# A new order of the attention's steps, and one row-sum step fewer per head pair

## The chip, the cores and the metric

The kernel runs on one core of a Trainium2 chip. A core has five engines, each with its own queue that is worked off in order: TensorE (PE in the profile; PEld are its weight loads), VectorE (DVE), ScalarE (ACT), GpSimd (POOL) and SyncE (SP), which here only issues DMAs. The metric is the time of one execution in microseconds on the device. Before the change it is 854.01 us, the median of three runs (853.5 to 854.5).

## The reference

Three parts follow one another: attention with a memory term over 4 batches of 8 heads, 576 positions and 64 columns, then two feed-forward layers over its output as 2304 tokens of 512 columns.

```python
scores = scale * np.matmul(q, k.transpose(0, 1, 3, 2))
scores = np.where(causal, -1000000000.0, scores)
scores = scores - scores.max(-1, keepdims=True)
a = np.exp(scores)
a /= a.sum(-1, keepdims=True) + 1e-09
local = np.matmul(a, v)
...
q_p = phi(q)                       # where(x > 0, x, exp(x) - 1) + 1
mem_out = (q_p @ M_prev) / (q_p @ z_prev + 1e-6)
return g * mem_out + (1 - g) * local     # g = sigmoid(beta), per head
```

The layers take weights of 64-bit floats, which arrive as pairs of 32-bit integers and are put together on the chip from exponent and mantissa.

## The kernel before

The attention works on 16 pairs of heads. Each pair runs through some seventy steps; a step is a method that issues a few instructions, nearly always on one engine. The steps that matter, with the pair as their argument n:

- lq, lk, lv, lz, cv_d: loads of q, k, v and M, z, and of raw weights, all issued on SP. tq_p, tk_p: transposes of q and k on TensorE; tq_h, tk_h (ScalarE) and tq_l, tk_l (VectorE, lines 393 and 406) split them into a high and a low part.
- s0_p to s4_p: scores on TensorE, block i having 128 (i + 1) columns, block 4 the 64 last rows of both heads. s0_m to s4_m: mask and row maximum on VectorE, reading PSUM (line 496). s0_e to s4_e: exponential with row sums on ScalarE (line 502). n01_r, n23_r, n4_r: a reduce and a reciprocal of a few columns on VectorE (lines 506 and 507). n0_p to n4_p: each block times its reciprocal on GpSimd, in place (line 513): two operations of 128, 256, 384 or 512 columns, one of 576 for block 4.
- ph_e: exp(q) on ScalarE (line 411). ph_m: minimum and maximum-plus on VectorE (lines 415 and 416, 640 columns, within SBUF). ph_g: times z on GpSimd (line 419). ph_r: row sum and reciprocal on VectorE (lines 427 and 428). ph_s: times the reciprocal on GpSimd (line 436). tf_p, tf_c: transpose and copy.
- g0_p, g1_p, t0_p to t3_p, tt_p, tc_p: transposes of the normalized blocks on TensorE; g1_c, tc_c (VectorE) and the other _c steps (ScalarE) copy them from PSUM. x0_m, x1_m, a00 to a14: products with M and v; x0_c, x1_c: copies of the result on VectorE.
- cv_a, cv_r, cv_b, cv_l: the conversion of raw weights of the first layer, beside the attention. For an even n these are exponent (line 194), bias on ScalarE (199), upper (202) and rest (209); for an odd n power (212, cv_a) and lower (215, cv_b). All but the bias are VectorE operations on 512 integers within SBUF.

Nothing is scheduled at run time. The lists HEAD, ORDER and TAIL at the top of the file give the order in which steps are issued, as name and pair. ORDER is repeated for a loop index and its numbers are relative to that; BODY is the loop's range, (1, 12), so eleven times. The order of the list is the order in each engine's queue; between engines only the data counts, so a step on GpSimd starts as soon as its own queue and its inputs allow, wherever the list has it. After the attention come the two layers, whose code the change does not touch; the first tiles of the first layer (xs0, xs1, h0 to h11, mx, ex, mu, sq, nm) stand in TAIL.

Of the kernel before, what the change touches and what calls it, by code (L numbers as in the profile page):

```python
# [22 lines left out]
HEAD = """
lq:0 ph_e:0 ph_m:0 tq_p:0 tq_h:0 tq_l:0 lk:0 lz:0 tk_p:0 tk_h:0 tk_l:0 s0_p:0 cv_h:0 s0_m:0 s4_p:0 lz:1
s4_m:0 lq:1 ph_g:0 ph_r:0 tq_p:1 tq_h:1 tq_l:1 s4_e:0 n4_r:0 ph_s:0 n4_p:0 s1_p:0 s1_m:0 s1_e:0 s3_p:0 s3_m:0
lk:1 tk_p:1 tk_h:1 s2_p:0 lz:2 s3_e:0 lq:2 tk_l:1 s3_p:1 s2_m:0 s2_e:0 n23_r:0 s0_e:0 n01_r:0 n1_p:0 cv_d:0
s0_p:1 n3_p:0 tf_p:0 n2_p:0 tf_c:0 s0_m:1 s4_p:1 lk:2 ph_e:1 s4_m:1 s4_e:1 g1_p:0 g1_c:0 ph_m:1 ph_g:1 lq:3
s0_e:1 s1_p:1 s1_m:1 s1_e:1 s2_p:1 s2_m:1 t3_p:0 tt_p:0 tt_c:0 t3_c:0 lv:0 ph_r:1 ph_s:1 tk_p:2 tk_h:2 cv_a:0  # L30
tq_p:2 cv_r:0 n4_r:1 n4_p:1 tk_l:2 tq_h:2 tc_p:0 lk:3 tc_c:0 n0_p:0 t1_p:0 t1_c:0 tq_l:2 tf_p:1 tf_c:1 t2_p:0
s4_p:2 s3_m:1 t2_c:0 n01_r:1 n0_p:1 s4_m:2 ph_e:2 cv_b:0 g0_p:0 lz:3 g0_c:0 t0_p:0 t0_c:0 s2_e:1 n1_p:1 s2_p:2
ph_m:2 ph_g:2 s1_p:2 s1_m:2 s0_p:2 s0_m:2 x0_m:0 a01:0 cv_d:1 x1_m:0 a00:0 s3_e:1 n23_r:1 n2_p:1 n3_p:1 s2_m:2
a14:0 a13:0 s1_e:2 a12:0 cv_p:0 a11:0 s4_e:2 a10:0 x1_c:0 ph_r:2 ph_s:2 tt_p:1 tt_c:1 tc_p:1 tc_c:1 tq_p:3
tq_h:3 tk_p:3 x0_c:0 t3_p:1 t1_p:1 s3_p:2 s0_e:2 t3_c:1
""".split()


TAIL = """
s3_m:13 cv_d:13 g0_p:12 s2_e:13 g0_c:12 lv:12 x1_m:12 a14:12 a13:12 n4_r:13 t1_c:12 cv_d:15 tq_l:14 s3_e:13 g1_p:12 g1_c:12  # L40
n01_r:13 n23_r:13 t0_p:12 n1_p:13 tk_h:14 tk_l:14 cv_a:12 n4_p:13 t0_c:12 x0_m:12 a01:12 cv_h:14 a00:12 n2_p:13 t2_p:12 x0_c:12
tf_p:13 t2_c:12 lv:14 s1_p:14 s1_m:14 s0_p:14 tf_c:13 a12:12 a11:12 a10:12 ph_e:14 s0_m:14 s0_e:14 s1_e:14 s2_p:14 n3_p:13
t2_p:13 t2_c:13 ph_m:14 x1_c:12 s2_m:14 s2_e:14 ph_g:14 ph_r:14 lz:15 xs0:0 tc_p:13 tc_c:13 s4_p:14 s4_m:14 t1_p:13 t1_c:13
cv_r:12 lq:15 tq_p:15 lk:15 s3_p:14 s3_m:14 t3_p:13 tq_h:15 t3_c:13 lv:13 tt_p:13 cv_b:12 cv_h:15 ph_s:14 tf_p:14 n01_r:14
n0_p:13 s4_e:14 n1_p:14 cv_r:13 tq_l:15 cv_l:12 g0_p:13 tt_c:13 g0_c:13 cv_h:13 x1_m:13 ph_e:15 a14:13 n0_p:14 g1_p:13 g1_c:13
cv_l:11 t0_p:13 tk_p:15 n4_r:14 n4_p:14 ph_m:15 ph_g:15 s3_e:14 tk_h:15 n23_r:14 n2_p:14 t0_c:13 n3_p:14 x0_m:13 cv_p:15 a13:13
a12:13 a11:13 tf_c:14 tk_l:15 cv_a:13 cv_b:13 a01:13 a00:13 x0_c:13 cv_d:14 cv_a:14 cv_r:14 a10:13 x1_c:13 s2_p:15 s0_p:15
s0_m:15 xs1:0 s4_p:15 tt_p:14 s4_m:15 tc_p:14 tt_c:14 tc_c:14 cv_b:14 s3_p:15 s3_m:15 s1_p:15 s1_m:15 s2_m:15 xs0:1 s0_e:15
t1_p:14 g0_p:14 x1_m:14 a14:14 g0_c:14 t2_p:14 s1_e:15 n01_r:15 n0_p:15 cv_p:12 ph_r:15 ph_s:15 cv_l:14 h0:0 h1:0 cv_r:15
t1_c:14 h2:0 h3:0 g1_p:14 h4:0 h5:0 h6:0 n1_p:15 cv_a:15 g1_c:14 h7:0 s2_e:15 h8:0 cv_p:14 s3_e:15 n23_r:15  # L50
cv_l:15 n2_p:15 cv_b:15 t2_c:14 s4_e:15 n4_r:15 t0_p:14 tf_p:15 tf_c:15 x0_m:14 a01:14 a00:14 cv_d:16 cv_a:16 cv_d:17 cv_a:17
cv_r:16 cv_b:16 t3_p:14 h0:1 n3_p:15 t0_c:14 xs1:1 n4_p:15 tt_p:15 h1:1 h9:0 tt_c:15 h10:0 cv_r:17 h11:0 cv_b:17
cv_p:17 lv:15 t2_p:15 mx:0 t2_c:15 h2:1 h3:1 cv_p:16 tc_p:15 t3_c:14 xs0:2 xs1:2 h4:1 tc_c:15 cv_h:12 ex:0
x0_c:14 g0_p:15 g0_c:15 cv_d:18 t1_p:15 t1_c:15 a13:14 cv_d:19 mu:0 a12:14 a11:14 a10:14 x1_c:14 cv_h:17 cv_l:17 cv_a:19
sq:0 g1_p:15 g1_c:15 cv_r:19 h5:1 h6:1 h7:1 cv_h:16 cv_l:16 cv_a:18 h8:1 h9:1 h10:1 cv_p:13 h11:1 cv_r:18
cv_b:19 t3_p:15 t3_c:15 nm:0 mx:1 cv_b:18 ex:1 t0_p:15 t0_c:15 mu:1 cv_p:18 cv_h:18 x0_m:15 a01:15 a00:15 x0_c:15
cv_p:19 cv_h:19 cv_l:18 cv_l:13 sq:1 x1_m:15 a14:15 a13:15 a12:15 a11:15 a10:15 cv_l:19 nm:1 x1_c:15
""".split()
# [1367 lines left out]
```

## Time and profile before

| | |
|---|---|
| median of three runs | 854.01 us |
| the profiled execution | 853.87 us, its span 852.1 us |
| TensorE busy | 829.5 us (97%) |
| VectorE busy | 636.8 us (75%) |
| ScalarE busy | 463.7 us (54%) |
| GpSimd busy | 478.4 us (56%) |
| head of the attention | 0 to 40.2 us |
| its eleven body periods | 40.2 to 170.8 us |
| its tail, with the first layer's first tiles | 170.8 to about 228.8 us |

The shares are means over stages of different kinds. The span runs from the first to the last instruction. In a timeline, a row is an instruction or several alike that follow each other; the number behind it in brackets is the time that the engine sat idle before it, and what released it.

### The profile page before, as it was taken

How to read it: one execution, taken by the hardware profiler on the slowest of the kernel's cores; microseconds unless marked ns; L12 is line 12 of the kernel's file. 1: busy time of each engine (PE TensorE's matmuls, PEld its weight loads, DVE VectorE, ACT ScalarE, POOL GpSimd, SP SyncE). 2: the span in 40 equal slices, each digit the busy share in tenths (PEclk: the TensorE clock that was granted, in tenths of full speed). 3: DMA queues.
4: the chain of work that ended last, by engine and by line, in shares of the span. 5: the costliest groups of instructions: out<-in, count | busy, mean ns of one | idle time of the engine just before them, and what ended most of it. 6: DMA issues, size and time to landing. Idle time of an engine off the chain costs nothing.

```text
span 852.1 us, 14791 instructions
## 1 busy us (share of the span) xinstructions
PE 829.5 (97%) x5020; PEld 730.3 (86%) x5020; DVE 636.8 (75%) x1340; ACT 463.7 (54%) x971; POOL 478.4 (56%) x563
## 2 busy tenths in 40 slices
...
GB/s 150 91 147 138 139 151 161 140 102 103 75 65 60 143 187 172 204 184 144 81 278 325 252 182 300 403 333 113 335 401 291 258 209 101 112 380 40 244 237 99
DMA packets 135835, 160.37 MB, mean 188 GB/s; under 512 B 69840, under 2 KB 103888, under 8 KB 135760
## 3 DMA queue, kind: packets, MB, share of 16 engines
...
q14 instruction: 35, 0.29, 0.1%
q10 hardware_dynamic: 320, 0.07, 0.0%
...
## 4 chain that ended last, share of the span: by engine, by line
PE 55%; DVE 6%; ACT 5%; POOL 4%; DMA 2%; issue 2%; SPq 0%; POOLq 0%; ACTq 0%; DVEq 0%
PE s L1169 17%; PE acc L1222 16%; PE g L1169 8%; PE po L816 7%; PE v L1169 4%; PE h L750 2%; ACT h L779 1%; DVE e L774 1%; DMA raw<-in_moe_w_val_dram 1%; ACT e L768 1%; DMA gv0s<-scrg 1%; POOL exwo L721 1%; POOL M L1016 1%; PE pl L797 1%; POOL M L1002 1%
## 5 line engine op out<-in xcount | busy, mean ns | idle before, releaser
L1222 PE MATMUL acc<-o,G 128*128 128x512 f32 x648 | 181.6, 390 | 0.2 <-DVE G L1188 0.2
L1207 POOL TENSOR_TENSOR vl<-vl,sg 128x384 f32<-128x384 f32 x36 | 37.1, 1030 | 204.4 <-ACT sg L1206 204.4
L1222 PEld LDWEIGHTS acc<-o,G 128*128 128x128 f32 x648 | 118.5, 188 | 10.3 <-DVE G L1188 0.7
L513 POOL TENSOR_SCALAR p<-p,first,cols 128x256 f32<-128x256 f32 (+4 forms) x142 | 105.7, 757 | 36.5 <-ACT p L502 14.3
L502 ACT ACTIVATE p<-p,nm 128x256 f32<-128x256 f32 (+4 forms) x144 | 83.1, 581 | 14.3 <-DVE nm L496 14.2
L750 PE MATMUL h<-wih,xs 128*128 128x512 f32 x288 | 84.5, 398 | 0.3 <-POOL xs L739 0.2
L1199 ACT ACTIVATE sg<-sg 128x384 f32<-128x384 f32 x36 | 18.9, 526 | 105.5 <-DVE sg L1198 105.4
L816 PE MATMUL po<-lnT,woh 128*128 128x384 f32 x288 | 73.5, 335 | 1.9 <-ACT woh L726 1.9
L1188 DVE TENSOR_TENSOR G<-vl,G 128x384 fp32r<-128x384 f32 x72 | 54.4, 755 | 21.5 <-ACT G L1185 21.4
L1185 ACT CAST G<-vl 128x384 fp32r<-128x384 f32 x72 | 37.1, 515 | 45.3 <-POOL vl L1207 36.4
L750 PEld LDWEIGHTS h<-wih,xs 128*128 128x128 f32 x288 | 52.3, 188 | 10.7 <-POOL xs L739 0.6
L1206 ACT ACTIVATE sg<-sg 128x384 f32<-128x384 f32 x36 | 18.9, 526 | 74.6 <-DVE sg L1205 74.5
L816 PEld LDWEIGHTS po<-lnT,woh 128*128 128x128 f32 x288 | 52.0, 188 | 2.6 <-ACT woh L726 2.3
L1002 POOL TENSOR_TENSOR M<-ex 128x256 f32<-128x256 f32 x48 | 42.3, 901 | 18.4 <-DVE ex L167 18.4
L816 PE MATMUL po<-lnT,wol 128*128 128x384 f32 x144 | 48.3, 335 | 0.2 <-DVE wol L727 0.2
L1193 DVE TENSOR_TENSOR u<-s,p 128x384 f32<-128x384 f32 x36 | 20.0, 557 | 36.6 <-PE s L1169 36.6
L750 PE MATMUL h<-wil,xs 128*128 128x512 f32 x144 | 44.9, 393 | 0.0
L1016 POOL TENSOR_TENSOR M<-M 128x256 f32<-128x256 f32 x48 | 43.8, 922 | 1.2
L1210 POOL TENSOR_TENSOR vl<-vl,sg 128x384 f32<-128x384 f32 x36 | 41.0, 1140 | 2.2 <-DVE vl L1209 0.5
L1209 DVE TENSOR_TENSOR vl<-v,u 128x384 f32<-128x384 f32 x36 | 20.1, 559 | 28.3 <-PE v L1169 28.2
L160 ACT ACTIVATE ex<-ex,consts 128x512 int32<-128x512 int32 x36 | 26.0, 722 | 28.0 <-DVE ex L150 28.0
L163 DVE SCALAR_TENSOR_TENSOR ex<-raw,ex 128x512 int32<-128x512 int32 x36 | 33.4, 928 | 10.2 <-ACT ex L160 10.2
...
## 6 DMA issues: line engine op xcount, KB each, us to landing
...
```

Source lines behind the costliest of these rows:

```text
L502: nc.scalar.activation(p, p, AF.Exp, bias=nm, scale=-1.0, accum_out=self.sum[n % 2][:, c, 0:1])
L513: eng.tensor_scalar(p, p, r["rs"][:, c : c + 1], og, ALU.mult, ALU.mult)
L750: lambda s=s, w=w, j=j: nc.tensor.matmul(ph[:, j * 512 : j * 512 + 512], xs[:, s, c], self.wi[c][w][:, j * 512 : j * 512 + 512], start=(c ...
L816: nc.tensor.matmul(self.po[g, m], w[:, m * P : m * P + P], L[x][c // 4][:, c % 4], start=(c == 0 and n == 0), stop=(c == NF1 - 1 and n == 2),)
L1002: nc.gpsimd.tensor_mul(out[:, sl], m[:, sl], e[:, sl])
L1016: ops[i][0](*ops[i][1:])
L1169: nc.tensor.matmul(po, W[:, a, c * P : c * P + P], xb[b][:, c], start=c + i == 0, stop=c == 1 and i == 2)
L1185: nc.scalar.copy(G[:, 0, hs[h]], vl[:, h])
L1188: nc.vector.tensor_sub(G[:, 1, hs[h]], vl[:, h], f32(G[:, 0, hs[h]]))
L1207: nc.gpsimd.tensor_mul(vl[:, 1], vl[:, 1], sg[:, 1])
L1210: nc.gpsimd.tensor_mul(vl[:, 0], vl[:, 0], sg[:, 0])
L1222: nc.tensor.matmul(po, G[:, x, sl], o[:, w], start=first and i == 0, stop=stop and i == 2)
```

## The change

The three lists are new, and BODY is (2, 12): ten repeats. In ORDER the numbers run from -2 to 2 where they ran from -1 to 3. HEAD has 113 steps in place of 152, TAIL 393 in place of 286. The steps n23_r and n4_r become one, n24_r, which sums and inverts columns 4 to 8 at once, so that n2_p to n4_p all wait for one step. On VectorE the new period is: s4_m, n24_r, x0_c, cv_b, x1_c, s0_m, s1_m, s2_m, ph_r, cv_l, tc_c, tq_l, n01_r, tk_l, s3_m, ph_m, g1_c, cv_a. On GpSimd: n3_p, n4_p, n2_p, ph_s, n1_p, n0_p, ph_g. Before it was, on VectorE: tq_l, cv_a, tk_l, n01_r, cv_l, g1_c, s3_m, n4_r, cv_b, s4_m, n23_r, ph_m, x1_c, x0_c, s0_m, s1_m, s2_m, ph_r, tc_c; on GpSimd: n0_p, n1_p, n4_p, n3_p, ph_g, n2_p, ph_s. HEAD and TAIL are left out here.

```diff
-BODY = (1, 12)
+BODY = (2, 12)
...
 ORDER = """
-tq_l:2 t2_p:0 tf_p:1 tk_h:2 t1_c:0 cv_a:0 g1_p:0 t2_c:0 s2_e:1 tk_l:2 cv_p:0 lv:0 n01_r:1 cv_l:-1 s4_p:2 cv_h:0
-g1_c:0 g0_p:0 ph_e:2 s3_m:1 cv_r:0 lq:3 s3_e:1 t0_p:0 x1_m:0 n4_r:1 t0_c:0 a14:0 a13:0 cv_b:0 g0_c:0 a12:0
-x0_m:0 n0_p:1 s4_m:2 n1_p:1 s4_e:2 a11:0 tf_c:1 a01:0 a10:0 n23_r:1 n4_p:1 n3_p:1 ph_m:2 a00:0 s0_p:2 s1_p:2
-s2_p:2 ph_g:2 x1_c:0 x0_c:0 s0_m:2 s3_p:2 n2_p:1 s0_e:2 s1_m:2 s1_e:2 t3_p:1 t3_c:1 cv_d:1 tq_p:3 tt_p:1 lk:3
-tq_h:3 s2_m:2 tc_p:1 tt_c:1 tk_p:3 ph_r:2 tc_c:1 t1_p:1 lz:3 ph_s:2
+a12:-2 s3_e:-1 s4_m:0 lk:1 n24_r:-1 t0_c:-2 a01:-2 a00:-2 a11:-2 a10:-2 x0_c:-2 n3_p:-1 lq:2 s0_p:0 cv_r:-2 n4_p:-1
+n2_p:-1 tf_c:-1 cv_b:-2 s1_p:0 s4_e:0 x1_c:-2 s2_p:0 cv_d:-1 s0_m:0 s1_m:0 s3_p:0 s0_e:0 s2_m:0 ph_r:0 ph_s:0 t3_p:-1
+cv_p:0 tt_p:-1 s1_e:0 cv_l:-2 lz:2 t3_c:-1 lv:1 cv_h:0 tt_c:-1 tq_p:1 t1_p:-1 tq_h:1 t1_c:-1 tc_p:-1 tc_c:-1 tk_p:1
+tq_l:1 tk_h:1 t2_p:-1 t2_c:-1 n01_r:0 tk_l:1 s3_m:0 g0_p:-1 tf_p:0 t0_p:-1 g0_c:-1 s4_p:1 n1_p:0 ph_e:1 g1_p:-1 x0_m:-1
+ph_m:1 g1_c:-1 x1_m:-1 cv_a:-1 s2_e:0 a14:-1 a13:-1 n0_p:0 ph_g:1
 """.split()
...
 
             sub = {
                 "n01_r": lambda n, r: self.n_r(n, r, 0, 4),
-                "n23_r": lambda n, r: self.n_r(n, r, 4, 8),
-                "n4_r": lambda n, r: self.n_r(n, r, 8, 9),
+                "n24_r": lambda n, r: self.n_r(n, r, 4, 9),
             }
             for i in range(5):
                 sub[f"s{i}_p"] = lambda n, r, i=i: self.s_p(n, r, i)
```

## Rows read from the trace of the kernel before

**Rows 1.** Table by stretch (length, busy PE, PEld, DVE, ACT, POOL, clock, DMA)

```profile
40.20:170.80 130.60, 129.97 (x1166) 100.00 (x1167) 127.68 (x400) 118.33 (x317) 103.46 (x122) 1.00 0.56 144
170.80:228.80 58.00, 55.48 (x405) 40.15 (x404) 50.51 (x137) 43.46 (x99) 34.83 (x44) 1.00 0.32 93
```

**Rows 2.** Timeline of VectorE in the body (start, duration, line, operation)

```profile
100.24 0.81 DVE L393 SCALAR_TENSOR_TENSOR q<-trq,q 128x640 fp32r<-128x640 f32 x1
...
100.97 0.84 DVE L194 TENSOR_SCALAR exh<-rawh 128x512 int32<-128x512 int32 x1
...
101.73 0.75 DVE L406 TENSOR_TENSOR kl<-trk,kh 128x576 fp32r<-128x576 f32 x1
...
102.67 0.40 DVE L222 COPY A<-t6a 128x256 f32<-128x256 f32 x1
...
102.98 0.68 DVE L496 CUSTOM_DVE_ANT_0 p<-x7s,mask 128x512 f32<-128x512 f32 x1
...
104.20 0.15 DVE L506 TENSOR_REDUCE first<-cols 128x1 f32<-128x2 f32 x1
...
104.38 0.16 DVE L507 RECIPROCAL first<-first 128x1 f32<-128x1 f32 x1
...
106.37 0.46 DVE L415 TENSOR_SCALAR E<-E 128x640 f32<-128x640 f32 x1
...
106.87 1.28 DVE L416 SCALAR_TENSOR_TENSOR E<-qt,E 128x640 f32<-128x640 f32 x1
...
108.07 0.81 DVE L222 COPY X<-x 128x320 f32<-128x320 f32 x2
...
112.11 0.81 DVE L393 SCALAR_TENSOR_TENSOR q<-trq,q 128x640 fp32r<-128x640 f32 x1
```

**Rows 3.** Timeline of ScalarE in the body

```profile
97.33 0.40 ACT L502 ACTIVATE p<-p,nm 128x128 f32<-128x128 f32 x1 [1.29 <-DVE nm L496]
...
109.20 0.40 ACT L502 ACTIVATE p<-p,nm 128x128 f32<-128x128 f32 x1 [0.79 <-DVE nm L496]
```

**Rows 4.** Timeline of VectorE elsewhere, the same kinds of operation

```profile
5.52 0.82 DVE L416 SCALAR_TENSOR_TENSOR E<-qt,E 128x640 f32<-128x640 f32 x1
...
34.19 0.87 DVE L416 SCALAR_TENSOR_TENSOR E<-qt,E 128x640 f32<-128x640 f32 x1
...
90.80 0.40 DVE L209 TENSOR_SCALAR midh<-midh 128x512 int32<-128x512 int32 x1
```

**Rows 5.** Timeline of GpSimd, head and body

```profile
34.38 1.11 POOL L513 TENSOR_SCALAR p<-p,first,cols 128x256 f32<-128x256 f32 x1
...
106.66 2.14 POOL L513 TENSOR_SCALAR p<-p,first,cols 128x512 f32<-128x512 f32 x2 [0.50 <-ACT Bt L222]
...
112.13 1.26 POOL L436 TENSOR_TENSOR E<-E,nr 128x640 f32<-128x640 f32 x1 [0.50 <-DVE nr L428]
...
114.82 3.21 POOL L513 TENSOR_SCALAR p<-p,first,cols 128x128 f32<-128x128 f32 x5 [1.43 <-ACT p L502]
```

**Rows 6.** Timeline of GpSimd, tail and later

```profile
181.06 1.57 POOL L419 TENSOR_TENSOR G<-E,zm 128x640 f32<-128x640 f32 x1 [0.75 <-DVE E L416]
...
191.05 1.73 POOL L419 TENSOR_TENSOR G<-E,zm 128x640 f32<-128x640 f32 x1
...
206.94 1.36 POOL L513 TENSOR_SCALAR p<-p,first,cols 128x576 f32<-128x576 f32 x1
...
363.64 0.74 POOL L1030 TENSOR_TENSOR M<-M,hi 128x256 fp32r<-128x256 f32 x1
```

**Rows 7.** Timeline of VectorE at those places

```profile
179.70 1.27 DVE L416 SCALAR_TENSOR_TENSOR E<-qt,E 128x640 f32<-128x640 f32 x1
...
191.40 1.93 DVE L215 SCALAR_TENSOR_TENSOR wil<-midh,exh 128x512 fp32r<-128x512 int32 x1
...
207.02 0.40 DVE L163 SCALAR_TENSOR_TENSOR qt<-raw,qt 128x256 int32<-128x256 int32 x1
...
363.76 1.17 DVE L163 SCALAR_TENSOR_TENSOR ex<-raw,ex 128x512 int32<-128x512 int32 x1 [0.51 <-ACT ex L160]
```

More of the change, by code (lines that the diff above doesn't have):

```diff
@@ L18 @@
 PSUM = bass.MemoryType.PSUM
-BODY = (1, 12)
+BODY = (2, 12)
 HEAD = """
[L26 to L34, printed above, removed]
@@ L35 @@
-tq_h:3 tk_p:3 x0_c:0 t3_p:1 t1_p:1 s3_p:2 s0_e:2 t3_c:1
+lq:0 tq_p:0 ph_e:0 lk:0 ph_m:0 lz:0 ph_g:0 tq_h:0 tq_l:0 tk_p:0 tk_h:0 tk_l:0 s0_p:0 ph_r:0 s1_p:0 s1_m:0
+s1_e:0 s2_p:0 s2_m:0 lq:1 ph_s:0 s2_e:0 tf_p:0 tf_c:0 s4_p:0 s0_m:0 cv_h:1 ph_e:1 lz:1 tq_p:1 cv_p:0 lz:2
+s4_m:0 ph_m:1 ph_g:1 s4_e:0 cv_d:0 tq_h:1 tq_l:1 lk:1 tk_p:1 tk_h:1 cv_p:1 s3_p:0 tk_l:1 s1_p:1 lv:0 s3_m:0
+s3_e:0 cv_h:0 s1_m:1 s1_e:1 s2_p:1 s2_m:1 n24_r:0 n4_p:0 s3_p:1 s0_p:1 s0_m:1 lq:2 s0_e:0 n01_r:0 s0_e:1 n2_p:0
+tq_p:2 lv:2 tq_h:2 ph_r:1 tt_p:0 tt_c:0 s4_p:1 lk:2 n3_p:0 t3_p:0 n0_p:0 n1_p:0 lq:3 s3_m:1 n01_r:1 tq_l:2
@@ L36 @@
+t1_p:0 t1_c:0 tk_p:2 lv:1 s4_m:1 t3_c:0 cv_a:0 lz:3 ph_s:1 tf_p:1 tk_h:2 tk_l:2 tc_p:0 x1_m:0 x0_m:0 s4_e:1
+n1_p:1 tc_c:0 a14:0 ph_e:2 a13:0 ph_m:2 ph_g:2 s2_e:1 t2_p:0 t2_c:0 g0_p:0 g0_c:0 n0_p:1 s4_p:2 g1_p:0 g1_c:0
+t0_p:0
 """.split()
 TAIL = """
-s3_m:13 cv_d:13 g0_p:12 s2_e:13 g0_c:12 lv:12 x1_m:12 a14:12 a13:12 n4_r:13 t1_c:12 cv_d:15 tq_l:14 s3_e:13 g1_p:12 g1_c:12
-n01_r:13 n23_r:13 t0_p:12 n1_p:13 tk_h:14 tk_l:14 cv_a:12 n4_p:13 t0_c:12 x0_m:12 a01:12 cv_h:14 a00:12 n2_p:13 t2_p:12 x0_c:12
@@ L42 @@
[L42 to L54, printed above, removed]
@@ L55 @@
-sq:0 g1_p:15 g1_c:15 cv_r:19 h5:1 h6:1 h7:1 cv_h:16 cv_l:16 cv_a:18 h8:1 h9:1 h10:1 cv_p:13 h11:1 cv_r:18
-cv_b:19 t3_p:15 t3_c:15 nm:0 mx:1 cv_b:18 ex:1 t0_p:15 t0_c:15 mu:1 cv_p:18 cv_h:18 x0_m:15 a01:15 a00:15 x0_c:15
-cv_p:19 cv_h:19 cv_l:18 cv_l:13 sq:1 x1_m:15 a14:15 a13:15 a12:15 a11:15 a10:15 cv_l:19 nm:1 x1_c:15
+s4_m:12 t0_c:10 lk:14 a12:10 a11:10 s3_e:11 n24_r:11 tf_c:11 s4_e:12 cv_l:13 s1_p:12 s1_m:12 s1_e:12 n3_p:11 s0_p:12 s0_m:12
+cv_l:15 s2_p:12 s2_m:12 a01:10 a00:10 s2_e:12 a10:10 x0_c:10 x1_c:10 lk:13 n4_p:11 tc_p:11 tc_c:11 tt_p:11 ph_r:12 ph_s:12
@@ new lines @@
+cv_l:10 tt_c:11 tq_p:13 tq_h:13 tq_l:13 lq:14 n2_p:11 t3_p:11 tk_p:13 lk:15 lz:14 tk_h:13 t3_c:11 tk_l:13 g0_p:11 g0_c:11
+cv_h:14 s3_p:12 s3_m:12 s0_e:12 tf_p:12 tf_c:12 n01_r:12 cv_h:15 s4_p:13 g1_p:11 n1_p:12 g1_c:11 s3_e:12 t2_p:11 tq_p:14 s4_m:13
+n24_r:12 n3_p:12 tq_h:14 tq_l:14 t1_p:11 ph_e:13 ph_m:13 lq:15 t1_c:11 t2_c:11 x1_m:11 a14:11 a13:11 x0_m:11 t0_p:11 cv_r:10
+cv_b:10 s1_p:13 s1_m:13 t0_c:11 s2_p:13 s2_m:13 s1_e:13 s2_e:13 s0_p:13 s0_m:13 ph_g:13 ph_r:13 a12:11 a11:11 a10:11 x1_c:11
@@ new lines @@
+n4_p:12 a01:11 tt_p:12 tt_c:12 t3_p:12 t3_c:12 n0_p:12 a00:11 x0_c:11 n2_p:12 s0_e:13 t2_p:12 t2_c:12 t1_p:12 t1_c:12 tk_p:14
+tk_h:14 cv_d:13 cv_p:15 cv_h:13 cv_a:11 tc_p:12 tc_c:12 ph_s:13 tf_p:13 tf_c:13 n01_r:13 t0_p:12 t0_c:12 g0_p:12 xs0:0 tk_l:14
+s2_p:14 cv_b:11 s2_m:14 s4_e:13 s3_p:13 n0_p:13 s3_m:13 ph_e:14 ph_m:14 s4_p:14 g0_c:12 s3_e:13 n24_r:13 cv_p:12 tq_p:15 n2_p:13
+cv_d:12 cv_a:12 ph_g:14 tq_h:15 tq_l:15 lv:14 g1_p:12 x0_m:12 g1_c:12 s4_m:14 s4_e:14 x1_m:12 a14:12 xs1:0 a13:12 a12:12
@@ new lines @@
+a11:12 a10:12 x1_c:12 tk_p:15 s0_p:14 s0_m:14 s1_p:14 lv:13 tk_h:15 tk_l:15 cv_d:11 s1_m:14 s2_e:14 a01:12 cv_r:11 a00:12
+x0_c:12 n4_p:13 tt_p:13 n3_p:13 tt_c:13 n1_p:13 t2_p:13 s4_p:15 ph_r:14 t2_c:13 cv_r:12 cv_b:12 tc_p:13 tc_c:13 g0_p:13 g0_c:13
+s4_m:15 s3_p:14 s3_m:14 t1_p:13 t1_c:13 t3_p:13 t3_c:13 ph_s:14 tf_p:14 t0_p:13 g1_p:13 g1_c:13 x1_m:13 a14:13 a13:13 xs0:1
+s3_e:14 n24_r:14 n3_p:14 ph_e:15 ph_m:15 x0_m:13 a01:13 cv_a:13 tf_c:14 a12:13 n4_p:14 lv:15 cv_r:13 t0_c:13 a11:13 a10:13
```

11 lines of the change are left out of this document (added).

## The prediction

> **What bounds the kernel now.** The table by stretch first. The eleven body periods fill 40.2 to 170.8 us, 130.6 us, and VectorE is busy for 127.68 of them; the tail of the attention follows, 58.0 us with VectorE busy for 50.51 [rows 1]. The page warns that a busy TensorE is not TensorE at its peak, so I looked next at VectorE's own timeline. One period there, from tq_l to the next tq_l, is 100.24 to 112.11, 11.87 us, and each row starts about 0.08 before the one ahead of it ends: VectorE has no idle time worth naming [rows 2]. ScalarE does: 1.29 us in one period and 0.79 in the next, waiting for VectorE [rows 3], so alone it would need 11.87 - 1.04 = 10.83. The body is bound by VectorE, and a microsecond taken from its period is worth ten (the new order has ten body periods; the eleventh goes to the tail), until ScalarE binds.
>
> **What the change removes.** Three terms, from start to start, since that is what the next operation sees.
>
> ph_m: its second operation takes 1.28 in the body and 0.82 at the start of the kernel, where GpSimd is idle [rows 2, 4]. In the body it meets n3_p, two operations of 512 columns in 2.14 [rows 5]. The new order puts n1_p and n0_p in front of ph_m, and the end of n0_p may reach into it; beside such narrow operations ph_m's took 0.87, and it was GpSimd that waited, 1.11 for 256 columns at 34.38 [rows 4, 5]. Gain 0.41 (0.46 if n0_p is done).
>
> cv_a: 100.97 to 101.73 is 0.76; a like operation on 512 integers with GpSimd nearly idle takes 0.40, so 0.32 from start to start [rows 2, 4]. It meets ph_s now: the ph_s of 112.13 [rows 5] stands one period earlier at 100.26, ends at 101.52, and cv_a ends 0.29 later, at 101.81. Possible gain 0.44.
>
> n24_r: a reduce and a reciprocal fall away, 104.20 to 104.54, about 0.27 after the overlap [rows 2]; five columns should cost what four do.
>
> Together 1.12, so 10.75 a period: ScalarE's 10.83 would bind, and with queues in order I would take 11.0. That is the change at its word.
>
> **What it adds.** An order holds nobody back; GpSimd starts whenever its inputs are there. So I laid the new order out from these rows, with the end of ph_m as zero. GpSimd's queue there is n1_p, n0_p, ph_g. n1_p is released by n01_r; from that to the end of ph_m VectorE has tk_l 0.67, s3_m 1.22 (102.98 to 104.20) and ph_m 0.50 + 0.79, together 3.18 [rows 2, 4]. n1_p and n0_p are four of the five operations that take 3.21 [rows 5]; the fifth, n4_p, is the widest, so the four take at most 2.5. GpSimd is idle when ph_m ends, and ph_g starts at once: a ph_g that waited for ph_m started at 181.06, 0.09 after the end at 180.97 [rows 6, 7].
>
> VectorE's next are g1_c, which reads PSUM, and then cv_a. A copy of g1_c's size takes 0.31 from start to start (102.67 to 102.98) [rows 2] and starts 0.08 early, so cv_a comes at +0.23, 0.14 behind ph_g. Who goes first? At 191.05 a ph_g was running, and a VectorE operation of 191.40 ended at 193.33, 0.55 after ph_g [rows 6, 7]. At 363.64 GpSimd led by 0.12, and VectorE's operation was held until 364.93, 0.55 after GpSimd's end. At 206.94 GpSimd led by 0.08 and VectorE won: 0.40, and GpSimd's 576 columns took 1.36 [rows 6, 7]. So the lead decides, between 0.08 and 0.12, and 0.14 goes to GpSimd. cv_a then ends 0.29 after ph_g, whose 1.57 end at +1.66; the next operation starts at +1.87, so cv_a costs 1.6 where it cost 0.76. That is +0.84: the collision that was removed comes back in another place, larger. Ends of this term: -0.44 (cv_a first) and +0.9. I take +0.84, as the row nearest in lead has it. Behind cv_a are queued s4_m and n24_r, and ScalarE (s4_e) and GpSimd (n3_p) wait for those.
>
> cv_b: n3_p is released by n24_r some 0.2 after it, and cv_b follows n24_r and x0_c, at +0.23 to +0.26: a lead of 0.03 to 0.06, which goes to VectorE by the row of 207.02. Taken 0. If it goes to GpSimd, cv_b waits for one 512-wide operation, 0.6 (ends: -0.05 and +0.7).
>
> The page "SBUF — State Buffer" of the Trainium skill (Who interferes with whom) says that the port pair which both engines share is locked for a whole instruction, and that whoever issues first has it. The rows of 191.40 and 363.76 agree; that of 207.02 doesn't, GpSimd had started 0.08 earlier. By the rule n3_p would be ahead of cv_b, which is rival B.
>
> A wait: tq_p of the next pair now stands behind tt_p on TensorE, tt_p waits for n4_p, and tq_h and tq_l wait for tq_p; s0_m to s2_m, ph_r and tc_c stand before tq_l on VectorE and nearly cover the 3.3 that n3_p and n4_p take (2.14 [rows 5] and some 1.2). Ends 0 and +0.35 a period; I take 0.1. Behind tq_l are queued n01_r, tk_l and s3_m, and ScalarE waits for s3_m.
>
> DMAs: lk issues three, lq and lv five, cv_d two, all on SP's queue, and all move to other places in the period. No VectorE row of the body names a DMA as its releaser [rows 2], and cv_d, the nearest to its use, stands some 8 us ahead of cv_a in the layout; cost 0, and if it lands late, ph_g only goes first the more surely.
>
> A body period: 11.87 - 0.41 - 0.27 + 0.84 + 0 + 0.1 = 12.13; ten of them +2.6 us.
>
> **Head and tail.** Both are written anew. The tail's VectorE is idle for 7.5 of 58 us [rows 1], so a collision there costs less than its length; the one of 191.40 waited 1.38. In the new tail most cv_ steps stand directly behind ph_m or another cv_ step, ahead of the GpSimd step that they would meet. Ends -6 and +4; I take -2.
>
> Sum: 853.87 (the profiled execution: span 852.1 and 1.8 around it) + 2.6 - 2 = 854.47; the median of the runs lies 0.14 above that execution: 854.6, say 854.5.
>
> **The rivals.**
> A, faster. cv_a comes first. For it: 0.14 us of lead is little. Against: ph_g would have to be late, and GpSimd has over half a microsecond to spare. The period is then 11.0, ten times -0.87, and -2: 843.
> B, slower. n3_p gets ahead of cv_b as well. Place: behind n24_r, each period; price 0.6; it decides from a lead of about 0.1, that is once TensorE's a00 holds x0_c back by 0.05. For it: the tie is closer than any row shows. Against: the row of 207.02. Ten times 0.6 on top: 860.5.
> C. That the change doesn't do what it says is the forecast itself: ph_m is freed and cv_a is caught.
>
> **How the numbers follow.** Forecast 0.42 (its own range 850 to 859), A 0.30, B 0.28. Less than 0.2%, 1.7 us, can't be told from no change here. Of the forecast 0.28 lies on the faster side, 0.38 within, 0.34 on the slower; A is nearly all faster, B all slower. Faster 0.41, same 0.17, slower 0.42. The range from 842 to 860 leaves out the far third of A and about half of B.
>
> **What would show it.** Right: ph_m's second operation near 0.85; cv_a at 1.5 or more in nearly every body period, ending 0.3 after a ph_g; 32 pairs of reduce and reciprocal in place of 48; a period near 12. A: cv_a at 0.40, ph_g starting after it, ScalarE without idle time, a period near 11. B: cv_b near 1.3. I am wrong in kind if VectorE shows waits that I don't name, or if head and tail move by more than 6 us.

## The result: slower, 866.7 us, and the profile after

After the change the median is 866.73 us (865.55 to 867.57, four runs); runs of the kernel before beside them gave 853.75. The ratio is 1.0150, 95% interval 1.0132 to 1.0168: slower by 1.5%, where 854.5 us and a range of 842 to 860 were forecast. The profiled execution took 867.57 us. Its span grew from 852.1 to 865.8; the page's first lines:

```profile
span 865.8 us, 14736 instructions
...
PE 835.9 (97%) x5020; PEld 734.5 (85%) x5020; DVE 637.3 (74%) x1308; ACT 465.9 (54%) x971; POOL 471.0 (54%) x563
```

VectorE is busy for as long as before (636.8 us then). The time is in waiting, and nearly all of it in the attention: the last copy of X starts at 225.28 before and at 238.41 after, 13.1 of the 13.7 us. The table by stretch says where. The answers are head, body and tail of the kernel after (length, then busy time of PE, PEld, DVE, ACT, POOL, clock, DMA), and below them the head of before; body and tail of before are [rows 1].

```profile
0.00:41.70 41.70, 28.00 (x165) 21.51 (x167) 23.40 (x84) 21.31 (x55) 18.29 (x37) 0.75 0.53 124
41.70:166.80 125.10, 121.01 (x1066) 91.97 (x1062) 118.95 (x346) 110.86 (x288) 88.88 (x110) 1.00 0.55 137
166.80:242.00 75.20, 72.59 (x558) 53.62 (x559) 66.86 (x186) 56.94 (x137) 46.83 (x59) 1.00 0.31 92
```

```profile
0.00:40.20 40.20, 30.95 (x213) 23.76 (x213) 29.05 (x110) 25.96 (x66) 23.85 (x42) 0.87 0.53 125
```

The stretches don't hold the same steps in both kernels (the new body has ten periods, the new head starts less), so lengths can't be set against each other, but VectorE's idle time can: length less its busy time. In the head it goes from 11.15 to 18.30 us, in the body from 2.92 to 6.15, in the tail from 7.49 to 8.34. That is 7.15 + 3.23 + 0.85; with 1.97 us more of busy time it makes the 13.2 by which the whole stretch grew (228.8 to 242.0). These sums understate the body: an operation that is held counts as busy, so the time for which the ten cv_a below are held stands in the busy time, where shorter ph_m and n24_r offset it.

One period of the body on VectorE, from one tq_l to the next, where [rows 2] had 11.87 us. Line numbers are 5 higher than before.

```profile
85.42 0.81 DVE L398 SCALAR_TENSOR_TENSOR q<-trq,q 128x640 fp32r<-128x640 f32 x1
...
88.33 0.68 DVE L420 TENSOR_SCALAR E<-E 128x640 f32<-128x640 f32 x1
89.04 0.82 DVE L421 SCALAR_TENSOR_TENSOR E<-qt,E 128x640 f32<-128x640 f32 x1
89.78 0.42 DVE L227 COPY A<-t4a 128x256 f32<-128x256 f32 x1
90.12 1.68 DVE L199 TENSOR_SCALAR exh<-rawh 128x512 int32<-128x512 int32 x1
91.72 0.75 DVE L501 CUSTOM_DVE_ANT_1 p<-sc,mask 128x576 f32<-128x576 f32 x1
...
92.39 0.15 DVE L511 TENSOR_REDUCE first<-cols 128x5 f32<-128x10 f32 x1
92.58 0.19 DVE L512 RECIPROCAL first<-first 128x5 f32<-128x5 f32 x1
...
92.98 0.68 DVE L207 SCALAR_TENSOR_TENSOR exh<-rawh,exh 128x512 int32<-128x512 int32 x1
...
97.72 0.29 DVE L227 COPY C<-t5d 128x128 f32<-128x128 f32 x1 [0.30 <-PE t5d L561]
97.93 0.81 DVE L398 SCALAR_TENSOR_TENSOR q<-trq,q 128x640 fp32r<-128x640 f32 x1
```

The period is 12.51 us. ph_m's second operation is free (0.82); its first, beside the end of n0_p, takes 0.68. cv_a takes 1.68 where it took 0.84, and so in all ten body periods. cv_b takes 0.68. tc_c waits 0.30 here, 0.60 in the periods without cv_l:

```profile
110.23 0.29 DVE L227 COPY C<-t6d 128x128 f32<-128x128 f32 x1 [0.60 <-PE t6d L561]
```

GpSimd beside it (the second row is n3_p, n4_p and half of n2_p together; the third, from a shorter window, is the first operation of n3_p alone):

```profile
89.95 1.57 POOL L424 TENSOR_TENSOR G<-E,zm 128x640 f32<-128x640 f32 x1 [1.29 <-DVE E L421]
92.94 3.49 POOL L518 TENSOR_SCALAR p<-p,first,cols 128x512 f32<-128x512 f32 x4 [1.43 <-DVE first L512]
...
92.94 1.29 POOL L518 TENSOR_SCALAR p<-p,first,cols 128x512 f32<-128x512 f32 x1 [1.43 <-DVE first L512]
```

ph_g starts 0.17 ahead of cv_a and ends 0.28 before it. n3_p starts 0.04 ahead of cv_b, and cv_b isn't held; it is n3_p's first operation that is long.

Last, ScalarE in the head. Rows marked ACTq are DMAs that stand in ScalarE's own queue.

```profile
11.96 0.49 ACT L507 ACTIVATE p<-p,nm 128x256 f32<-128x256 f32 x1
...
14.56 2.57 ACTq L348 DMA_DIRECT2D qt<-in_q_dram  x2
17.18 0.61 ACT L507 ACTIVATE p<-p,nm 128x384 f32<-128x384 f32 x1 [4.63 <-DMA kt<-in_k_dram]
```

ScalarE stands still for 4.63 us. The two DMAs are the small loads of q for pair 1. They belong to step lq, and for the first two pairs ScalarE issues them, in both kernels: the list of steps ahead of the prediction, which has all loads on SP, isn't right here. In the kernel before they went out at 9.02, together, and took 1.12:

```profile
9.02 1.12 ACTq L343 DMA_DIRECT2D qt<-in_q_dram  x2
```

### The profile page after: what moved, and what is told of

Its sections match the earlier page's. It is cut to its first block, busy times and chain, and to the rows that moved or that the text cites. A ratio compares the mean times of both kernels' runs of the same rounds, so it can differ in the third digit from the quotient of the medians.

```text
span 865.8 us, 14736 instructions
## 1 busy us (share of the span) xinstructions
PE 835.9 (97%) x5020; PEld 734.5 (85%) x5020; DVE 637.3 (74%) x1308; ACT 465.9 (54%) x971; POOL 471.0 (54%) x563
## 4 chain that ended last, share of the span: by engine, by line
PE 64%; DVE 13%; POOL 8%; ACT 6%; DMA 4%; issue 2%; SPq 2%; ACTq 0%; POOLq 0%; DVEq 0%
PE s L1173 16%; PE acc L1226 16%; PE g L1173 8%; PE po L820 7%; PE v L1173 4%; PE h L754 3%; POOL p L518 3%; PE x L588 2%; DMA kt<-in_k_dram 2%; DVE p L501 2%; ACT h L783 1%; DVE e L778 1%; DMA raw<-in_moe_w_val_dram 1%; ACT e L772 1%; DVE exh L199 1%
## 5 line engine op out<-in xcount | busy, mean ns | idle before, releaser
L518 POOL TENSOR_SCALAR p<-p,first,cols 128x128 f32<-128x128 f32 (+4 forms) x142 | 96.8, 695 | 41.6 <-DVE first L512 26.6
L507 ACT ACTIVATE p<-p,nm 128x384 f32<-128x384 f32 (+4 forms) x144 | 82.8, 576 | 25.1 <-DVE nm L501 15.3
L424 POOL TENSOR_TENSOR G<-E,zm 128x640 f32<-128x640 f32 x16 | 25.4, 1588 | 29.2 <-DVE E L421 23.9
```

The source lines that it names most:

```text
L507: nc.scalar.activation(p, p, AF.Exp, bias=nm, scale=-1.0, accum_out=self.sum[n % 2][:, c, 0:1])
L518: eng.tensor_scalar(p, p, r["rs"][:, c : c + 1], og, ALU.mult, ALU.mult)
```

## The experiments

Each ran beside the kernel before; differences in this section are medians against the kernel before that ran beside it. For the kernel after that difference is 13.0 us. The diffs show only the part of a list around the step that moved.

**cva_first: cv_a directly behind ph_m.**

```diff
-ph_m:1 g1_c:-1 x1_m:-1 cv_a:-1 s2_e:0
+ph_m:1 cv_a:-1 g1_c:-1 x1_m:-1 s2_e:0
```

> The changed kernel with one step moved in the body: cv_a:-1 stands directly behind ph_m:1, in front of g1_c, so VectorE goes from one operation to the next without the 0.31 us in which ph_g gets ahead. Nothing is added or left out. Theory (ph_g holds cv_a for 1.2 us a period): cv_a falls from 1.68 to about 0.45, ph_g starts about 0.3 later, the body period falls from 12.51 to 11.2 to 11.5, and ten periods give 856.7 to 853.5 us, 10 to 13 less than the changed kernel. Rival 1 (cv_a is long but something else sets the period, such as the wait behind n4_p at tc_c): cv_a falls, tc_c's wait grows from 0.45 to about 1.6, the time stays within 2 us of 866.7. Rival 2 (with ph_g later, n3_p starts beside cv_b and takes the port): cv_b goes from 0.68 to about 1.3, the gain is only 5 us.

855.17 us, 1.3 above before (ratio 1.0009, 0.9995 to 1.0024): 11.6 of the 13.0 us go with one moved step. The period is 11.50. VectorE, then GpSimd:

```profile
108.59 0.82 DVE L421 SCALAR_TENSOR_TENSOR E<-qt,E 128x640 f32<-128x640 f32 x1
109.34 0.42 DVE L199 TENSOR_SCALAR exh<-rawh 128x512 int32<-128x512 int32 x1
...
111.40 1.14 DVE L207 SCALAR_TENSOR_TENSOR exh<-rawh,exh 128x512 int32<-128x512 int32 x1
```

```profile
109.50 1.67 POOL L424 TENSOR_TENSOR G<-E,zm 128x640 f32<-128x640 f32 x1 [1.29 <-DVE E L421]
111.23 1.95 POOL L518 TENSOR_SCALAR p<-p,first,cols 128x512 f32<-128x512 f32 x2
```

cv_a directly behind ph_m leaves GpSimd no gap: 0.42. ph_g now starts 0.16 behind it. Rival 1 is out. Rival 2 is there in part: n3_p now starts 0.17 ahead of cv_b, and cv_b takes 1.14 in every period from the third on; but the wait at tc_c fell to 0.29 in every other period, so the period still lost 1.0. n3_p's first operation, which comes first now, takes 0.77 where it took 1.29:

```profile
111.23 0.77 POOL L518 TENSOR_SCALAR p<-p,first,cols 128x512 f32<-128x512 f32 x1
```

**load_later: cv_d:0 in the head behind lk:2.**

```diff
-ph_g:1 s4_e:0 cv_d:0 tq_h:1 tq_l:1 lk:1
+ph_g:1 s4_e:0 tq_h:1 tq_l:1 lk:1
...
-tt_p:0 tt_c:0 s4_p:1 lk:2 n3_p:0
+tt_p:0 tt_c:0 s4_p:1 lk:2 cv_d:0 n3_p:0
```

> The changed kernel with one step moved in the head: cv_d:0 (two loads of 512 KB each for the first weight conversion) stands behind lk:2 in place of in front of lk:1; the body is that of the changed kernel. Theory (these loads hold back lk:1 and lv:0, and the two small loads that ScalarE issues for lq:1, at 14.56 and 16.66 us, so ScalarE stands still for 4.6 us): the two small loads are issued some 4 us earlier, the second ph_m starts near 16 in place of 19.84, and the time falls by 3 to 6 us, to 861 to 864. Rival (the head is long because of its order of work, not of the loads): 866 to 867, with the same VectorE idle time of about 18 us before 41.7.

860.85 us, 7.0 above before (1.0076, 1.0054 to 1.0097): 6.0 of the 13.0. The first tq_l of the body comes at 42.44 in place of 47.81. ScalarE's queue:

```profile
11.79 0.47 ACTq L347 DMA_DIRECT2D qt<-in_q_dram  x1
...
11.94 0.49 ACT L506 ACTIVATE p<-p,nm 128x256 f32<-128x256 f32 x1
12.30 0.61 ACTq L347 DMA_DIRECT2D qt<-in_q_dram  x1
...
12.96 0.61 ACT L506 ACTIVATE p<-p,nm 128x384 f32<-128x384 f32 x1 [0.44 <-DVE nm L500]
```

The loads of cv_d:0 are the cause. The way by which they act was open still; two runs at the end of this section tell it.

TensorE's clock comes into it as well. From 16.6 to 22.3 us the kernel after is granted 0.50 (the lower level, 1.2 GHz) and load_later 1.00 (2.4 GHz); in the 7.7 us up to 16.4, TensorE had been busy for 4.37 in the first and for 6.46 in the second. By itself the clock does less than the loads: tc_later, the next run, has the head of the kernel after unchanged, but its second stretch at 0.50 ends at about 37.5 us in place of 39.4. Its g1_c, VectorE's last step of the head, comes at 39.63 in place of 40.73, where load_later has it at 35.38, and its time is no lower. How much of the 6.0 us came back by way of the clock isn't told apart.

**tc_later and tc_free: the wait at tc_c.**

```diff
-t3_p:-1 cv_p:0 tt_p:-1 s1_e:0
+t3_p:-1 cv_p:0 tq_p:1 tt_p:-1 s1_e:0
...
-tt_c:-1 tq_p:1 t1_p:-1 tq_h:1
+tt_c:-1 t1_p:-1 tq_h:1
...
-tc_p:-1 tc_c:-1 tk_p:1 tq_l:1 tk_h:1
+tc_p:-1 tk_p:1 tq_l:1 tc_c:-1 tk_h:1
```

> The changed kernel with two steps moved in the body: on TensorE tq_p:1 stands in front of tt_p:-1, and on VectorE tc_c:-1 stands behind tq_l:1. Theory (tc_c's wait of 0.3 and 0.6 us in turn, behind tt_p, which waits for n4_p, is on the path): no wait at tc_c, the body period falls by 0.3 to 0.45, ten periods give 862 to 864 us. Rival 1 (the wait is slack that moves to the next step): s3_m or ph_m wait as long, 866 to 867. Rival 2 (tq_p in front of tt_p delays n4_p's readers and GpSimd's or ScalarE's turn): slower, 868 or more.

In tc_free tt_c stands behind tq_h as well:

```diff
-t3_c:-1 lv:1 cv_h:0 tt_c:-1 t1_p:-1 tq_h:1 t1_c:-1
+t3_c:-1 lv:1 cv_h:0 t1_p:-1 tq_h:1 tt_c:-1 t1_c:-1
```

> The changed kernel with three steps moved in the body: tq_p:1 stands in front of tt_p:-1 on TensorE and tc_c:-1 behind tq_l:1 on VectorE, as in the run before, and tt_c:-1 now behind tq_h:1 on ScalarE. cv_a stays caught. Theory (in the run before, tq_h stood behind tt_c in ScalarE's queue, so the wait only moved from tc_c to tq_l, 0.36 and 0.64 in turn): with tt_c out of the way tq_h ends 0.5 earlier, neither tc_c nor tq_l waits, the body period goes from 12.51 to 12.0 to 12.1, and ten periods give 862 to 863 us. Rival (the time is set by the exponentials behind s0_m, which begin late because cv_a is late, so that every cut of this wait comes back as a wait of s3_m, ph_m or n01_r for ScalarE): 866 to 867, with a wait of about 0.4 at another VectorE step.

867.22 us (1.0149, 1.0120 to 1.0178) and 868.42 us (1.0163, 1.0143 to 1.0182): nothing gained. Both times the theory failed and the rival held. VectorE of tc_later, two periods, then of tc_free:

```profile
97.38 0.82 DVE L398 SCALAR_TENSOR_TENSOR q<-trq,q 128x640 fp32r<-128x640 f32 x1 [0.36 <-ACT q L394]
...
109.91 0.82 DVE L398 SCALAR_TENSOR_TENSOR q<-trq,q 128x640 fp32r<-128x640 f32 x1 [0.64 <-ACT q L394]
```

```profile
111.00 0.76 DVE L411 TENSOR_TENSOR kl<-trk,kh 128x576 fp32r<-128x576 f32 x1 [0.64 <-ACT kh L227]
```

The wait moved from tc_c to tq_l and from there to tk_l, at its full size, and the period stayed at 12.53 and 12.57. So it isn't the wait of one badly placed step. As I read the rows, from n24_r the work goes to GpSimd (n3_p, n4_p), TensorE (tt_p) and ScalarE, and comes back to VectorE ahead of s3_m; that way takes longer than what VectorE has to do beside it, in all three places that the step that waits has had.

**merge_alone: the kernel before with n24_r in its body.**

```diff
-x1_m:0 n4_r:1 t0_c:0
+x1_m:0 t0_c:0
...
-a10:0 n23_r:1 n4_p:1 n3_p:1 ph_m:2
+a10:0 n24_r:1 n4_p:1 n3_p:1 ph_m:2
```

> The kernel before with one edit: in the body n4_r falls away and n24_r stands in the place of n23_r (one reduce and one reciprocal over five columns in place of two of each); order, head and tail are those of before. Theory (VectorE binds the body of the kernel before, and a pair costs 0.27 us): eleven periods give -3.0, 850.8 us. Rival 1 (n4_p is released later by the merge, GpSimd's n4_p and n3_p end later and the gain is lost): 853 to 854. Rival 2 (the overlap with ph_m, n3_p against ph_m's second operation, shifts): between 848 and 857, seen at the second operation of ph_m (1.28 before).

856.92 us, 3.1 above before (1.0034, 1.0018 to 1.0051): slower. The theory failed; the merge alone costs 0.27 a period (12.14). What rival 1 named is there, at more than its price; rival 2 isn't (ph_m's second operation takes 1.33, 1.28 before). GpSimd, then VectorE:

```profile
104.62 1.95 POOL L513 TENSOR_SCALAR p<-p,first,cols 128x128 f32<-128x128 f32 x4 [1.44 <-ACT p L502]
108.33 3.03 POOL L513 TENSOR_SCALAR p<-p,first,cols 128x576 f32<-128x576 f32 x3 [1.77 <-DVE first L507]
```

```profile
106.43 0.69 DVE L202 SCALAR_TENSOR_TENSOR exh<-rawh,exh 128x512 int32<-128x512 int32 x1 [0.50 <-ACT exh L199]
...
112.92 0.83 DVE L427 TENSOR_REDUCE nr<-G 128x10 f32<-128x650 f32 x1 [0.17 <-POOL G L419]
```

n4_p (576 columns) used to run with n0_p and n1_p, released by n4_r; now GpSimd is idle for 1.77 and has n4_p and n3_p together behind n24_r. ph_g ends later, ph_r waits 0.17 for it in most periods, and cv_b, which the pair in front of it had covered, waits 0.30 to 0.50 for the bias in every other period.

**n4_early: the merge taken back in the kernel after.**

```diff
-lk:1 n24_r:-1 t0_c:-2
+lk:1 n23_r:-1 t0_c:-2
...
-cv_r:-2 n4_p:-1 n2_p:-1
+cv_r:-2 n2_p:-1
...
-s2_m:0 ph_r:0 ph_s:0 t3_p:-1
+s2_m:0 ph_r:0 n4_r:0 ph_s:0 n4_p:0 t3_p:-1
```

(n4_r:1 and n4_p:1 stand in HEAD; n23_r:11 in TAIL, without n4_p:11.)

> The changed kernel with the merge of the row sums undone for the body alone: n23_r stands in the place of n24_r, n4_r behind ph_r of its own pair and n4_p behind ph_s, a period earlier than before, where GpSimd waits for n01_r; cv_a stays caught and the order is otherwise that of the changed kernel. Theory (tc_c's wait of 0.3 and 0.6 us in turn comes from n4_p, which stands behind n3_p and n24_r): no wait at tc_c for tt_p; VectorE does one pair more, 0.27; the body period goes from 12.51 to 12.3, the time to 864 to 865.5. Rival 1 (the exponentials behind the caught cv_a set the period, so the wait comes back at tq_l or tk_l): period 12.5 to 12.8, 867 to 870. Rival 2 (n4_p beside tq_l and n01_r is slow or slows them): ph_g starts late, cv_a goes first in some periods, under 860.

860.54 us (1.0081, 1.0063 to 1.0100), 5.7 us less than the kernel after. Theory and rival 2 each came true in part, and the time lies between theirs: the wait at tc_c is down to 0.17 in every other period, and also in every other period GpSimd was late and cv_a went first. GpSimd's ph_g and VectorE's cv_a, two periods:

```profile
87.35 1.56 POOL L427 TENSOR_TENSOR G<-E,zm 128x640 f32<-128x640 f32 x1 [0.76 <-DVE E L424]
...
99.76 1.79 POOL L427 TENSOR_TENSOR G<-E,zm 128x640 f32<-128x640 f32 x1
```

```profile
87.52 1.67 DVE L202 TENSOR_SCALAR exh<-rawh 128x512 int32<-128x512 int32 x1
...
99.73 0.41 DVE L220 TENSOR_SCALAR exh<-exh 128x512 int32<-128x512 int32 x1
```

GpSimd 0.17 ahead: cv_a 1.67. GpSimd 0.03 behind: cv_a 0.41, and ph_g pays 0.2. The period is 11.88 on the mean; five free cv_a in ten make 0.63, which is the whole of the difference. So the end of the wait and the pair more cancel within what can be read here, and their sizes aren't told apart.

**cvab, cvab_load and all: cv_b moved without cv_r.**

```diff
-s4_m:0 lk:1 n24_r:-1 t0_c:-2
+s4_m:0 lk:1 n24_r:-1 cv_b:-2 t0_c:-2
```

> The kernel with cv_a behind ph_m, and one step more: cv_b:-2 directly behind n24_r:-1, in front of x0_c. Theory (once cv_a is free, ph_g ends later, n3_p starts 0.17 ahead of cv_b and holds it to 1.14 in each body period; two VectorE operations in direct succession leave GpSimd no gap): cv_b goes back to 0.68, the period from 11.50 to 11.0 to 11.1, and the time to 850 to 851.5 us. Rival 1 (n3_p, put off by 0.35, makes n4_p and tt_p late by as much): the wait at tc_c grows from 0.15 on the mean to 0.5, 854 to 855. Rival 2 (n24_r's small reciprocal does leave a gap): cv_b unchanged, 855.

> The kernel with cv_a behind ph_m and cv_b behind n24_r, and in the head cv_d:0 behind lk:2. Theory (head and body add up): 5 to 6 us less than the same body with the old head, 844.5 to 846, faster than the kernel before by 1%. Rival (a faster body meets the limit of something later, so that the head's gain is lost): over 849.

> All moves together: cv_a behind ph_m, cv_b behind n24_r, cv_d:0 behind lk:2 in the head, and tq_p, tt_c, tc_c placed so that the next pair's q does not stand behind n4_p. Theory (what is left of the wait at tc_c, 0.15 to 0.5 us a period, goes): ScalarE's 10.83 then sets the period, 842 to 844 us, 1 to 3 less than without the last move. Rival (ScalarE already sets it): the same as without the last move, 844.5 to 846.

(The old place of cv_b falls away. All three also have the edit of cva_first, cvab_load and all that of load_later, and all has the moves of tc_free as well.)

869.85, 866.03 and 870.03 us (1.0191, 1.0144 and 1.0194). These tell nothing of the theories: cv_b overtook cv_r in the lists, so the upper halves are stored without the bias, and cv_r has to wait for that store, as ScalarE of cvab shows:

```profile
95.62 0.72 ACT L204 ACTIVATE exh<-exh,consts 128x512 int32<-128x512 int32 x1 [3.56 <-DMA wih<-exh]
```

**cva_load, cvab2_load and n4_cvab2_load: the moves put together.** cva_load has the edits of cva_first and load_later. cvab2_load also has

```diff
-a12:-2 s3_e:-1 s4_m:0 lk:1 n24_r:-1 t0_c:-2
+a12:-2 s3_e:-1 cv_r:-2 s4_m:0 lk:1 n24_r:-1 cv_b:-2 t0_c:-2
```

(the old places of both fall away), and n4_cvab2_load the edit of n4_early on top.

> The changed kernel with two moves: cv_a:-1 directly behind ph_m:1 in the body, cv_d:0 behind lk:2 in the head. Theory (the two gains, 11.5 and 5.9 us by the runs before, lie in different stretches and add up): 849 to 850 us, 0.5% faster than the kernel before. Rival (the later load or the faster body collide where body and head meet): 851 or more.

> The same two moves, and cv_r:-2 directly behind s3_e:-1 on ScalarE and cv_b:-2 directly behind n24_r:-1 on VectorE, so that cv_b still comes after cv_r (in the three earlier runs with cv_b moved it did not: cv_r came after it, so it computed with the exponent's bias missing, and cv_r had to wait for the store of cv_b's result). Theory (cv_b, in direct succession to n24_r, is in front of n3_p): cv_b at 0.68 in place of 1.14, the period from 11.50 to 11.0 to 11.1, 845 to 846 us. Rival 1 (n3_p put off by 0.35 makes tt_p and tc_c late): 849 to 850. Rival 2 (the reciprocal of n24_r leaves GpSimd a gap): cv_b at 1.2 and more.

> All of it: cv_a behind ph_m, cv_r and cv_b moved together, cv_d:0 later in the head, and n4_r and n4_p taken out of the merge and a period earlier. Theory (VectorE has no other wait then; a pair more costs 0.27, what is left of tc_c's wait goes): 844 to 848 us, within 2 us of the kernel without the last step. Rival (n4_p in front of n1_p and n0_p makes ph_g late, cv_a is free anyway, but ph_r waits): 850 or more.

850.84, 850.73 and 851.00 us beside 853.24: 0.9969 (0.9958 to 0.9981), 0.9965 (0.9950 to 0.9980) and 0.9970 (0.9958 to 0.9983). All three are faster than the kernel before. The two gains of the first experiments (11.6 and 6.0) add up to 15.4 of 17.6, so cva_load missed its 849 to 850 by a little. Moving cv_b did what it should at its place (0.75 in place of 1.14), but the period only went from 11.50 to 11.36, not to 11.0 to 11.1, and the time missed the theory's 845 to 846. Rival 1's mechanism is there, small: tc_c waits 0.39 in place of 0.29 in every other period. n4_cvab2_load missed its 844 to 848 too and came to its rival's "850 or more". There cv_b, though directly behind the reciprocal of n23_r, is held to 1.12 in every other period, by a ph_g that had started 1.0 us earlier. VectorE, then GpSimd:

```profile
71.09 0.18 DVE L515 RECIPROCAL first<-first 128x4 f32<-128x4 f32 x1
71.18 1.12 DVE L223 SCALAR_TENSOR_TENSOR wil<-midh,exh 128x512 fp32r<-128x512 int32 x1
```

```profile
70.18 1.56 POOL L427 TENSOR_TENSOR G<-E,zm 128x640 f32<-128x640 f32 x1
```

In cvab2_load the attention ended 1.2 us earlier than in cva_load (last copy of X at 221.24 in place of 222.44), which the times, each known to some 0.1%, don't show. The table from 60 to 150 us, of before and of cvab2_load:

```profile
60.00:150.00 90.00, 89.66 (x806) 69.11 (x802) 88.35 (x278) 81.39 (x217) 71.28 (x83) 1.00 0.58 147
```

```profile
60.00:150.00 90.00, 90.00 (x842) 71.33 (x840) 86.18 (x273) 84.97 (x227) 70.04 (x88) 1.00 0.60 151
```

VectorE now has 3.8 us of slack in 90, ScalarE 5.0, TensorE none. So TensorE is the likely limit at 11.36; no run took work from it, and a busy TensorE isn't one at its peak, so this isn't shown.

**small_loads_sync and k_first: how the loads of cv_d:0 act.** In the first, lq's two small loads of pair 1 are issued by SyncE; in the second, cv_d:0 stands directly behind lk:1.

```diff
-                (nc.scalar if n < 2 else nc.sync).dma_start(
+                (nc.scalar if n < 1 else nc.sync).dma_start(
```

```diff
-ph_g:1 s4_e:0 cv_d:0 tq_h:1 tq_l:1 lk:1 tk_p:1
+ph_g:1 s4_e:0 tq_h:1 tq_l:1 lk:1 cv_d:0 tk_p:1
```

> The changed kernel with one edit: the two small loads of q for pair 1, which ScalarE issues in the changed kernel, are issued by SyncE behind that pair's other loads; cv_d:0 stays in front of lk:1. Theory A (ScalarE stands still for 4.6 us because these two instructions stand in its queue while the rings are full of cv_d:0's packets): ScalarE goes on at 12.5, the second ph_m starts near 15 in place of 19.84, and the time falls by 4 to 6 us, to 861 to 863. Theory B (lk:1, which lands at 16.6 behind the two loads of 512 KB, is what the head waits for, whoever issues the small loads): tk_p:1 starts at 20.2 as before or at best at 17, and the time falls by 0 to 2 us.

> The changed kernel with one step moved in the head: cv_d:0 directly behind lk:1 in place of in front of it; the small loads stay on ScalarE. Theory A (ScalarE's two issues are held while cv_d:0's packets move): they are still held, since the loads of cv_d:0 start only 2 us later, and the time falls by 0 to 2 us. Theory B (lk:1 is late): lk:1 lands 4 us earlier and the time falls by 4 to 6 us, to 861 to 863.

861.45 us (1.0082, 1.0059 to 1.0106) and 864.89 us (1.0118, 1.0095 to 1.0141): 7.3 and 10.7 above before, so 5.7 and 2.3 less than the kernel after. That is theory A by the times (k_first 0.3 over its 0 to 2), though k_first does it in another way than A said. Its ScalarE wasn't held; the loads went out at 11.80 and 12.32 and were late in landing. The DMA list from 8 to 18 us (count, KB each, median us to landing), of k_first and then of load_later, and the transposes of k_first's second q, which read them:

```profile
qt<-in_q_dram ACTq DMA_DIRECT2D x2, 16.0 KB, 6.0
```

```profile
qt<-in_q_dram ACTq DMA_DIRECT2D x2, 16.0 KB, 2.0
```

```profile
18.42 0.47 PE L383 MATMUL trq<-ident,qt 128*128 128x128 f32 x1 [2.13 <-DMA mt<-in_M_prev_dram]
```

(The releaser named is another transfer that ended about then; trq reads qt.) So two loads of 16 KB are what the head waits for. Issued by ScalarE after 11 us they meet the 1 MB of cv_d:0, which goes out at 7.7 in the kernel after: either their issue is held and ScalarE with it (4.63 us), or they land late. SyncE's queue has them in front of cv_d:0, where neither happens (the second q then stands ready at 16.69, where ScalarE begins tq_h), though lk:1 still comes behind cv_d:0 there (its transposes at 16.57 wait 0.43 for it). The page "DMA: Bandwidth & Descriptors" of the Trainium skill (Issuing engines are not separate DMA queues) says that DMAs of all engines run interleaved on the same 16 engines; the 6.0 us of k_first agree.

**best2: cvab2_load with the small loads on SyncE.**

> The kernel with cv_a behind ph_m, cv_r and cv_b moved together and cv_d:0 later, and the small loads of q for pair 1 issued by SyncE. Theory A: with cv_d:0 out of the way the two issues are no longer held, so nothing changes, 850 to 851.5. Theory B: likewise. Rival: ScalarE's queue is still held for some tenths there, and the time falls by 1 us.

850.26 us beside 854.17 (0.9952, 0.9936 to 0.9969), the same as cvab2_load within what can be told. Its ratio is the lowest of all: 0.5% under the kernel before and, by the two ratios (0.9952 and 1.0150), 2% under the kernel after.

## Why the prediction was wrong

- **cv_a caught by ph_g: right.** +0.84 a period was forecast; from start to start it went from 0.76 to 1.60, +0.84. The lead was 0.17 where 0.14 was worked out, and GpSimd was first in ten periods of ten. cva_first shows that this collision alone is worth 11.6 us. With cv_a first the period there is 11.50, so rival A's condition alone would not have brought its 11.0: cv_b was held then, and tc_c still waited.
- **ph_m freed: right, over-sized.** 0.25 gained (1.70 to 1.45 from start to start) where 0.41 was taken: its second operation is at 0.82, but n0_p ends in its first.
- **n24_r: the instructions went as forecast** (32 pairs in place of 48, five columns in 0.15 and 0.19); from start to start these steps take 0.33 a period less, where 0.27 was taken. That taking them away must gain anything was not safe: merge_alone lost 0.27 a period in the old order. By its rows the step that fell away had released GpSimd's n4_p and covered cv_b's bias, which was worth more than its own length.
- **cv_b against n3_p: right.** A lead of 0.03 to 0.06 was worked out and given to VectorE; it was 0.04, and cv_b took 0.68. Rival B didn't occur. GpSimd pays in its place (1.29 for n3_p's first operation, 0.77 in cva_first); the 2.14 that the prediction took for n3_p had room for that. The page "SBUF — State Buffer" of the Trainium skill (Who interferes with whom) says that whoever issues first has the port pair for the whole instruction. The two periods of n4_early agree (1.67 and 0.41); cv_b after n3_p's 0.04 of lead doesn't, if the start in the trace is the issue.
- **The wait behind n4_p: the mechanism right, the size wrong.** It was put at +0.1 (ends 0 and 0.35); it is 0.30 and 0.60 in turn, 0.45 on the mean, outside the ends, and at tc_c, not tq_l. I counted VectorE's steps as cover for GpSimd's 3.3 us (it took 2.85, from 92.94 to 95.79) and left out that TensorE and ScalarE come behind that, with s0_e, s1_e, t3_c and tt_c in ScalarE's queue. Without its wait the period is 12.06, where the other terms of the sum gave 12.03 (which is partly luck: ph_m's missing 0.16 is made up by n24_r's 0.06, by cv_b, 0.71 to 0.60 in every other period, and by x0_c); with it, 12.51 against 12.13. Over ten periods that is 3.8 us of the miss.
- **Head and tail: the step that failed.** -2 us was taken (ends -6 and +4). By difference they cost some +6.5: 12.9 us in all (866.73 less the 853.87 on which the sum stands) less ten times 0.64. The tail's part is small (0.85 of idle time). The head I had weighed as a question of collisions on VectorE, and the moved loads only for the body, where no VectorE row waits for a DMA in the kernel after either. I also had all of them on SP's queue, which is not so for lq of the first two pairs. In the head cv_d:0 moved from behind lq:2 to in front of lk:1, its 1 MB met two small loads in ScalarE's queue, and moving it behind lk:2 returned 6.0. Head and tail together are some 8.5 us of the miss of 12.2, and what the prediction named as being wrong in kind; the 2.5 that load_later doesn't account for stay open.

Apart from the wait behind n4_p (0.35 a period), the terms that were read from rows at the place where they act came out within 0.16 a period; the one that was taken for head and tail as a whole, with no row of the head's queues behind it, was off by some 8.5 us.
